# An RWKV-6 layer with a mixture-of-depths block: a rank sum, two early products and one PSUM bank moved

## The chip, the cores and the metric

The kernel runs on one core of one Trainium2 chip. The time is that of one execution on the device in microseconds. The profile is of one further execution and has a span of its own (205.5 us here), a little shorter than the time measured for the whole run.

## The reference, cut to what matters

There are two blocks, one after the other, all in fp32. The first is a linear attention with a decay for every element:

```python
for t in range(S):                       # B, H, S, D = 4, 8, 768, 48
    cur = einsum('bhd,bhe->bhde', u * k[t], v[t])
    y[t] = einsum('bhd,bhde->bhe', r[t], state + cur)
    state = w[t][..., None] * state + einsum('bhd,bhe->bhde', k[t], v[t])
```

Its output becomes x of shape (4, 768, 384). The second block scores each row, sends the 128 rows with the highest scores of each batch through a small network, and adds the result to them:

```python
scores = einsum('bsd,d->bs', x, w_gate)
top = argpartition(-scores[b], 128)[:128]
h = maximum(x[b, top] @ w1, 0)           # w1 384 x 1024
out[b, top] = x[b, top] + sigmoid(scores[b, top])[:, None] * (h @ w2)
```

All other rows of out are those of x.

## The kernel before, in words

The 768 steps of each batch are cut into 6 chunks of 128, so there are 24 chunks. Each chunk handles all 8 heads at once, two heads in the 128 partitions after a transpose. A chunk passes through these stages, each a small function:

- `decays_t` and `scans`: TensorE transposes w (ps_w), and two scans on DVE turn it into running products of the decays, to the right (`right`) and to the left (`left`) of each step.
- `inputs_t` and `scaled`: TensorE transposes k and r into PSUM (ps_t), and DVE multiplies them by `right` and `left`. The products are called K and R. `first_left` on ACT sets one column of `left`.
- `scores`, `masked`, `outputs_t`: K against R (ps_s), a mask on DVE (sc), then sc against v and the carried state against R (ps_yt), which ACT copies out as yt.
- `back`, `carry_products`, `carry`: K is transposed back, copied by ACT (kt), and multiplied with v (ps_kv) into the state that the next chunk needs.
- `own_products`, `own_weights`, `own_values`, `own_results`: the term of each step with itself, on POOL and ACT (rk, own, vo).
- `rows_out`, `row_products`, `row_sums`: yt is transposed into rows (ps_y), vo is added, the row goes out, and its score is summed.
- `compared`: each row's score is compared with those of the other rows of its batch (`ahead`, in bf16), and DVE leaves three counts a row in `lost`: its own comparisons in columns 0 and 1, and a fixed count of later rows in column 2.

When the last chunk of a batch is compared, `mixture(b)` finds each row's rank. 21 bf16 matmuls (L504) sum `ahead` over the partitions with weight -1 into a PSUM tile ps_r; one fp32 matmul with the identity (L509) adds `lost` to it; DVE sums three columns into `rank` (L514). Six comparisons make `pick`, a matmul turns it into row numbers (ps_i, idx), and POOL gathers the rows by an indirect DMA (xe). They are transposed (ps_x, xeT). `forward` is the network: ps_h over two halves of four blocks, each copied by ACT with a Relu into `hid` (L596), then ps_f = hid times w2 in 8 accumulating products (L602), then DVE's `ye` (L609) and an indirect DMA out (L612).

The order of the instructions on each engine is written out by hand. `turn(i)` works on several chunks at once: the scans of chunk i+2, K and R of chunk i+1, scores and outputs of chunk i, rows of chunk i-1. `mix` and `fed` insert pieces of `mixture` and `forward` between them. Each engine runs its own list in order, and waits on the others by semaphores. After the last turn the remaining pieces follow one another; the list `ended` marks this.

PSUM is full: psT holds two tiles and psW, psY, psK and psM one each, and psS one double tile. A tile can be written again when its last reader is done. In `forward`, after the turns, the first half of ps_h takes psY and the second half psM (L587); ps_f takes psM (L600). `warm(n)` runs n matmuls on zeros in psM, which keeps TensorE busy while the first loads arrive.

Of the kernel before, what the change touches and what calls it, by code (L numbers as in the profile page):

```python
# [10 lines left out]
FP32 = mybir.dt.float32  # L11
# [4 lines left out]
ALU = mybir.AluOpType  # L16
AX = mybir.AxisListType

L = 128
# [19 lines left out]
def kernel(  # L39
# [271 lines left out]
    def scaled(t, name, by):  # L311
        out = t[name] = lev.tile([L, HP, L], FP32, tag=name, name=name)
        nc.vector.tensor_mul(out, t.pop(name + "t"), t.pop(by))  # L313

    def own_products(t):
        n = t["n"]
        rk = t["rk"] = lev.tile([L, H, D], FP32, tag="rk", name="rk")
        nc.gpsimd.tensor_mul(rk, r_bufs[n % NBUF][:, :, 0:D], k_bufs[n % NBUF][:, :, 0:D])  # L318
# [172 lines left out]
    def mixture(b):  # L491

        every, ahead, lost = against[b]
        pool, tag = (psK, "kv") if ended else (psY, "y")  # L500
        ps = pool.tile([L, NCH, 3], FP32, tag=tag, name="ps_r")
        for e in range(NCH):
            for c in range(e + 1):
                nc.tensor.matmul(  # L504
                    ps[:, c, 0:1], ahead[:, e, c * L:(c + 1) * L], minus,
                    start=(e == 0), stop=False, skip_group_check=True,
                )
        against.pop(b)
        nc.tensor.matmul(  # L509
            ps.rearrange("p c k -> p (c k)"), ident, lost.rearrange("p c k -> p (c k)"),  # L510
            start=False, stop=True, skip_group_check=True,
        )
        rank = mod.tile([L, NCH], FP32, name="rank", bufs=2)
        nc.vector.tensor_reduce(out=rank, in_=ps, axis=AX.X, op=ALU.add)  # L514

        for gi, (c0, n) in enumerate(groups):

            pick = mod.tile([L, NCH, L], BF16, name="pick")
            at = rank
            if c0 > 0:  # L520
                at = mod.tile([L, NCH], FP32, name="at")
                nc.vector.tensor_scalar_add(out=at, in0=rank, scalar1=float(-c0))
            for c in range(NCH):
                nc.vector.tensor_scalar(
                    out=pick[:, c, :], in0=slots, scalar1=at[:, c:c + 1], scalar2=None,
                    op0=ALU.is_equal,
                )
            yield "half"
            ps = psK.tile([L, 2], FP32, tag="kv", name="ps_i")
            for c in range(NCH):  # L530
                nc.tensor.matmul(
                    ps, pick[:, c, :], ids[:, b, c, :], start=(c == 0), stop=(c == NCH - 1)
                )
            while len(picked) + len(feed) > 1:
                fed(1)
            idx = mod.tile([L, 1], UINT32, name="idx", bufs=2)
            nc.vector.tensor_scalar(
                out=idx, in0=ps[:, 0:1], scalar1=ps[:, 1:2], scalar2=float(b * S),
                op0=ALU.add, op1=ALU.max,
            )  # L540
            rows = views[b][0:b + 1].rearrange("b s c -> (b s) c")
            where = bass.IndirectOffsetOnAxis(ap=idx[0:n, 0:1], axis=0)
            xe = mod.tile([L, C], FP32, name="xe", bufs=2)
            if n < L:
                nc.vector.memset(xe, 0.0)
            nc.gpsimd.indirect_dma_start(
                out=xe[0:n], out_offset=None, in_=rows, in_offset=where,
                bounds_check=(b + 1) * S - 1, oob_is_err=False,
            )
            yield "end"  # L550
            yield "mid"

            ps = psT.tile([L, NDC, L], FP32, tag="t", name="ps_x")
            for dc in range(NDC):
                nc.tensor.transpose(ps[:, dc, :], xe[:, dc * L:(dc + 1) * L], ident)  # L555
            xeT = mod.tile([L, NDC, L], FP32, name="xeT", bufs=2)
            nc.scalar.copy(out=xeT, in_=ps)  # L557
            gate = mod.tile([L, 1], FP32, name="gate", bufs=2)
            gated = []
            picked.append((b, n, idx, xe, xeT, gate, gated))  # L560
            yield "end"


            scr = mod.tile([L, C], FP32, name="scr_x")
            nc.gpsimd.tensor_mul(scr, xe, wg_bc)
            yield "half"
            own = mod.tile([L, 1], FP32, name="own", bufs=2)
            nc.scalar.activation(out=scr, in_=scr, func=AF.Copy, accum_out=own)
            nc.scalar.activation(out=own, in_=own, func=AF.Exp, scale=-1.0)  # L569
            yield "end"  # L570
            nc.vector.tensor_scalar(
                out=gate, in0=own, scalar1=1.0, scalar2=3e38, op0=ALU.add, op1=ALU.min
            )
            nc.vector.reciprocal(out=gate, in_=gate)
            gated.append(True)
            yield "end"

    def forward(b, n, idx, xe, xeT, gate, gated):

        load_weights(len(weights) - NFC // 2)
        hid = mod.tile([L, NFC, L], FP32, name="hid")
        for f0 in range(0, NFC, 4):

            pool, tag = (psY, "y") if ended and f0 % 8 == 0 else (psM, "m")  # L587
            ps = pool.tile([L, 4, L], FP32, tag=tag, name="ps_h")
            for q in range(4):
                for dc in range(NDC):  # L590
                    nc.tensor.matmul(  # L591
                        ps[:, q, :], w1[:, dc, (f0 + q) * L:(f0 + q + 1) * L],
                        xeT[:, dc, :], start=(dc == 0), stop=(dc == NDC - 1),
                    )
                if q == 3:
                    nc.scalar.activation(out=hid[:, f0:f0 + 4, :], in_=ps, func=AF.Relu)  # L596
                yield q == 3

        load_weights(len(weights))
        ps = psM.tile([L, C], FP32, tag="m", name="ps_f")  # L600
        for fc in range(NFC):
            nc.tensor.matmul(  # L602
                ps, hid[:, fc, :], w2[:, fc, :], start=(fc == 0), stop=(fc == NFC - 1)
            )
            yield fc == NFC - 1
        while not gated:
            mix()
        ye = mod.tile([L, C], FP32, name="ye", bufs=2)
        nc.vector.scalar_tensor_tensor(  # L609
            out=ye, in0=ps, scalar=gate, in1=xe, op0=ALU.mult, op1=ALU.add  # L610
        )
        nc.gpsimd.indirect_dma_start(  # L612
            out=views[b][0:b + 1].rearrange("b s c -> (b s) c"),
            out_offset=bass.IndirectOffsetOnAxis(ap=idx[0:n, 0:1], axis=0),
            in_=ye[0:n], in_offset=None,
            bounds_check=(b + 1) * S - 1, oob_is_err=False,
        )
        yield True
# [46 lines left out]
    def turn(i):  # L665
        soon = i >= N - 1
        step(first_left, i + 1)
        step(own_products, i + 1)
        step(scores, i)
        step(own_values, i)  # L670
        step(carry, i - 1, work.get(i))
        step(scaled, i + 1, "K", "right")
        step(own_weights, i + 1)
        if soon:
            step(masked, i)
        if i == N - 1:
            sums.extend(check_sums())
        if i < N:
            step(compared, i - 2)
        if not soon:  # L680
            step(masked, i)
        step(back, i)
        if i == 0:
            warm(6)
        mix(place="half")
        step(rows_out, i - 1, soon)
        step(row_scores_soon if soon else row_products, i - 1)
        step(own_results, i)
        fed_in_turn(PIECES // 2, 2 if i >= N - 1 else 1)
        step(inputs_t, i + 1, "R", r_bufs)  # L690
        if i == -1:
            warm(4)
        step(scaled, i + 1, "R", "left")
        step(decays_t, i + 2)
        mix(place="mid")
        if i == -2:
            warm(2)
        step(range_check, i + 2)
        step(outputs_t, i)
        step(carry_products, i)  # L700
        fed_in_turn(PIECES - PIECES // 2, 1 if i == N - 1 else 0)
        if i == N - 1:
            step(compared, i - 1)
        step(inputs_t, i + 2, "K", k_bufs)
        if i == -2:
            warm(1)
        if not soon:
            step(row_sums, i - 1)
        step(scans, i + 2)
        if 0 <= i - 2 < N - 1 and chunks[i - 2][1] == NCH - 1:  # L710
            mixing.append([mixture(chunks[i - 2][0]), "end"])
        mix(place="end")
        if i > -2:
            loads(i + 5)
        if i in WEIGHT_TURNS:
            load_weights(1)
# [93 lines left out]
```

## Time and profile before

The time was 207.15 us, the median of three runs (207.13 to 207.45).

| engine | busy us of the 205.5 us span | instructions |
|---|---|---|
| TensorE matmul (PE) | 192.5 | 2303 |
| TensorE weight load (PEld) | 156.7 | 2303 |
| VectorE (DVE) | 161.2 | 350 |
| ScalarE (ACT) | 123.4 | 642 |
| GpSimd (POOL) | 133.2 | 165 |

A busy share is an average over the whole span. The start, some 16 us, is taken up by the first loads; then come the turns, until about 177 us; then the last two batches' networks. The profile has several views: the chain of work that ended last, which follows the span back from its end through whatever released each step; the timeline of each engine, with the start and length of each group of instructions and, in brackets, the idle time before it and what ended that; and groups of instructions by line and by tile.

### The profile page before, as it was taken

How to read it: one execution, taken by the hardware profiler on the slowest of the kernel's cores; microseconds unless marked ns; L12 is line 12 of the kernel's file. 1: busy time of each engine (PE TensorE's matmuls, PEld its weight loads, DVE VectorE, ACT ScalarE, POOL GpSimd, SP SyncE). 2: the span in 40 equal slices, each digit the busy share in tenths (PEclk: the TensorE clock that was granted, in tenths of full speed). 3: DMA queues.
4: the chain of work that ended last, by engine and by line, in shares of the span. 5: the costliest groups of instructions: out<-in, count | busy, mean ns of one | idle time of the engine just before them, and what ended most of it. 6: DMA issues, size and time to landing. Idle time of an engine off the chain costs nothing.

```text
span 205.5 us, 6424 instructions
## 1 busy us (share of the span) xinstructions
PE 192.5 (94%) x2303; PEld 156.7 (76%) x2303; DVE 161.2 (78%) x350; ACT 123.4 (60%) x642; POOL 133.2 (65%) x165
## 2 busy tenths in 40 slices
PE   7899999989899899999999999999999999999880
PEld 3568888868687688897887898897787898877740
DVE  5999999999999968989868888979868984941010
ACT  7177877768754866787445776786545776310300
POOL 6266898886858896669638898668738896122101
PEclk9999999999999999999999999999999999999997
DMA  5999999999999999988992894997553211101101
GB/s 109 186 163 179 165 180 211 221 205 143 249 178 257 201 183 217 236 193 182 210 158 80 153 217 94 137 171 150 124 83 91 56 49 41 48 33 40 40 6 43
DMA packets 105671, 29.20 MB, mean 142 GB/s; under 512 B 100512, under 2 KB 104864, under 8 KB 105632
## 3 DMA queue, kind: packets, MB, share of 16 engines
q1 hardware_dynamic: 105120, 27.14, 74.1%
q0 software_dynamic: 512, 1.57, 2.6%
q8 instruction: 20, 0.33, 0.7%
q14 instruction: 19, 0.16, 0.3%
HBM read 23.20 MB, written 5.51 MB: 140 GB/s over the span
## 4 chain that ended last, share of the span: by engine, by line
PE 81%; SPq 4%; DVE 4%; DMA 3%; ACT 2%; POOL 2%; issue 2%; POOLq 0%; DVEq 0%; ACTq 0%
PE ps_t L242 12%; PE ps_s L342 11%; PE ps_h L591 11%; PE ps_f L602 11%; PE ps_yt L375 10%; PE ps_yt L383 5%; PE ps_y L242 5%; PE ps_w L242 5%; PE ps_kv L437 5%; SPq L135 3%; PE ps_e L478 3%; DMA k_buf<-in_k_dram 3%; PE ps_r L504 1%; ACT rk L327 1%; PE ps_x L555 1%
## 5 line engine op out<-in xcount | busy, mean ns | idle before, releaser
L327 ACT ACTIVATE rk<-rk 128x48 f32<-128x48 f32 x192 | 43.7, 230 | 0.0
L327 ACT ACTIVATION_READ_ACCUMULATOR rk<-rk 128x1 f32 x192 | 36.2, 189 | 0.0
L407 POOL TENSOR_TENSOR x<-x,vo 128x384 f32<-128x384 f32 x22 | 22.1, 1006 | 21.2 <-ACT x L405 21.0
L266 DVE TENSOR_TENSOR_SCAN left<-ps_w,from_left 128x511 f32<-128x511 f32 x24 | 30.7, 1280 | 0.9
L388 ACT COPY yt<-ps_yt 128x512 f32<-128x512 f32 x24 | 14.1, 586 | 28.1 <-PE ps_yt L383 24.9
L255 DVE TENSOR_TENSOR_SCAN right_buf<-ps_w,from_right 128x511 f32<-128x511 f32 x24 | 29.1, 1210 | 1.7 <-PE ps_w L242 1.7
L350 DVE TENSOR_TENSOR sc<-ps_s,before_f 128x1024 f32<-128x1024 f32 x24 | 29.3, 1219 | 0.8 <-PE ps_s L342 0.8
L318 POOL TENSOR_TENSOR rk<-r_buf,k_buf 128x384 f32<-128x384 f32 x24 | 24.1, 1006 | 6.8 <-DMA r_buf<-in_r_dram 6.8
L342 PE MATMUL ps_s<-R,K 48*128 48x128 f32 x384 | 27.9, 285 | 0.3 <-ACT yt L388 0.2
L375 PE MATMUL ps_yt<-sc,v_buf 128*64 128x128 f32 x384 | 26.3, 278 | 1.4 <-PE ps_w L242 1.2
L342 PEld LDWEIGHTS ps_s<-R,K 48*128 48x128 f32 x384 | 23.3, 187 | 3.9 <-issue 2.7
L321 POOL TENSOR_TENSOR rk<-rk,u_bc 128x384 f32<-128x384 f32 x24 | 24.2, 1007 | 2.5 <-DMA u_bc<-in_u_dram 1.9
L591 PE MATMUL ps_h<-xeT,w 128*128 128x128 f32 x192 | 25.5, 280 | 0.2 <-ACT hid L596 0.2
L375 PEld LDWEIGHTS ps_yt<-sc,v_buf 128*64 128x64 f32 x384 | 20.6, 136 | 5.7 <-issue 2.7
L602 PE MATMUL ps_f<-w,hid 128*128 128x384 f32 x64 | 23.9, 500 | 0.7 <-ACT hid L596 0.7
L591 PEld LDWEIGHTS ps_h<-xeT,w 128*128 128x128 f32 x192 | 22.9, 192 | 1.6 <-ACT xeT L557 0.5
L412 POOL TENSOR_TENSOR scr<-x,wg_bc 128x384 f32<-128x384 f32 x22 | 22.0, 1001 | 1.7
L333 POOL TENSOR_TENSOR vo<-v_buf,own 128x384 f32<-128x384 f32 x24 | 20.0, 832 | 1.6 <-ACT rk L327 1.3
L313 DVE TENSOR_TENSOR K<-ps_t,right_buf 128x512 f32<-128x512 f32 x24 | 16.4, 682 | 4.9 <-PE ps_t L242 4.9
L313 DVE TENSOR_TENSOR R<-ps_t,left 128x512 f32<-128x512 f32 x24 | 16.5, 686 | 3.9 <-ACT own L569 1.6
L242 PE MATMUL ps_w<-ident,w_buf 128*128 128x128 f32 x96 | 15.3, 283 | 0.9 <-ACT every L489 0.7
L302 ACT ACTIVATE junk<-w_buf,high 128x384 f32<-128x384 f32 x24 | 15.1, 630 | 1.6 <-DMA w_buf<-in_w_dram 1.6
(102 smaller groups left out, 347.9 us busy)
## 6 DMA issues: line engine op xcount, KB each, us to landing
k_buf<-in_k_dram SPq DMA_DIRECT2D x24, 192.0 KB, 5.3
r_buf<-in_r_dram SPq DMA_DIRECT2D x24, 192.0 KB, 5.2
v_buf<-in_v_dram SPq DMA_DIRECT2D x24, 192.0 KB, 5.2
out_dram<-x SPq DMA_DIRECT2D x24, 192.0 KB, 3.1
w_buf<-in_w_dram SPq DMA_DIRECT2D x23, 192.0 KB, 4.6
w<-in_moe_w_dram SPq DMA_DIRECT2D x3, 512.0 KB, 5.2
w<-in_moe_w_dram SPq DMA_DIRECT2D x4, 384.0 KB, 5.4
w_buf<-in_w_dram SPq DMA_DIRECT2D x2, 96.0 KB, 2.8
```

The costliest lines, as they stand in the source:

```text
L242: nc.tensor.transpose(ps[:, j, :], src(j), ident)
L255: nc.vector.tensor_tensor_scan(out=flat[:, W - 2::-1], data0=wt[:, W - 1:0:-1], data1=from_right.rearrange("p j t -> p (j t)")[:, W - 2::- ...
L266: nc.vector.tensor_tensor_scan(out=left.rearrange("p j t -> p (j t)")[:, 1:W], data0=wt[:, 0:W - 1], data1=start.rearrange("p j t -> p (j ...
L313: nc.vector.tensor_mul(out, t.pop(name + "t"), t.pop(by))
L318: nc.gpsimd.tensor_mul(rk, r_bufs[n % NBUF][:, :, 0:D], k_bufs[n % NBUF][:, :, 0:D])
L321: nc.gpsimd.tensor_mul(t["rk"], t["rk"], u_bc)
L327: nc.scalar.activation(out=rk[:, h, :], in_=rk[:, h, :], func=AF.Copy, accum_out=o[:, h:h + 1])
L342: nc.tensor.matmul(ps[:, q, j, :], t["K"][rows, j, :], t["R"][rows, j, :], start=True, stop=True,)
L350: nc.vector.tensor_mul(t["sc"].rearrange("p q j t -> p (q j) t"), ps.rearrange("p q j t -> p (q j) t"), _heads(before_f, 2 * HP),)
L375: nc.tensor.matmul(ps[half(c), j % 2, j // 2, :], vt[:, 2 * j + q, :], t["sc"][:, q, j, :], start=(j < 2), stop=(old is None), skip_group_ ...
L591: nc.tensor.matmul(ps[:, q, :], w1[:, dc, (f0 + q) * L:(f0 + q + 1) * L], xeT[:, dc, :], start=(dc == 0), stop=(dc == NDC - 1),)
L602: nc.tensor.matmul(ps, hid[:, fc, :], w2[:, fc, :], start=(fc == 0), stop=(fc == NFC - 1))
```

## The change

There are four edits. The products K of the first two chunks are taken from DVE: ACT copies the transposed k out of PSUM, and POOL multiplies it. They are also issued earlier within the turn. The matmul that added `lost` goes; DVE sums `lost` by itself and then adds ps_r, which shrinks to one column a chunk and ends its accumulation with the last group of L504. The last batch's ps_f takes the psY bank in place of psM, so that it need not wait for the reader of the second ps_h. Two of the four warm matmuls ahead of the first chunk go. The arithmetic is the same.

```diff
+    def scaled_aside(t, name, by):
+        out = t[name] = lev.tile([L, HP, L], FP32, tag=name, name=name)
+        src = setup.tile([L, HP, L], FP32, name="src")
+        nc.scalar.copy(out=src, in_=t.pop(name + "t"))
+        nc.gpsimd.tensor_mul(out, src, t.pop(by))
...
-        ps = pool.tile([L, NCH, 3], FP32, tag=tag, name="ps_r")
+        ps = pool.tile([L, NCH], FP32, tag=tag, name="ps_r")
         for e in range(NCH):
             for c in range(e + 1):
                 nc.tensor.matmul(
-                    ps[:, c, 0:1], ahead[:, e, c * L:(c + 1) * L], minus,
-                    start=(e == 0), stop=False, skip_group_check=True,
+                    ps[:, c:c + 1], ahead[:, e, c * L:(c + 1) * L], minus,
+                    start=(e == 0), stop=(e == NCH - 1), skip_group_check=True,
                 )
         against.pop(b)
-        nc.tensor.matmul(
-            ps.rearrange("p c k -> p (c k)"), ident, lost.rearrange("p c k -> p (c k)"),
-            start=False, stop=True, skip_group_check=True,
-        )
         rank = mod.tile([L, NCH], FP32, name="rank", bufs=2)
-        nc.vector.tensor_reduce(out=rank, in_=ps, axis=AX.X, op=ALU.add)
+        nc.vector.tensor_reduce(out=rank, in_=lost, axis=AX.X, op=ALU.add)
+        nc.vector.tensor_add(rank, ps, rank)
...
-        ps = psM.tile([L, C], FP32, tag="m", name="ps_f")
+        pool, tag = (psY, "y") if b == B - 1 else (psM, "m")
+        ps = pool.tile([L, C], FP32, tag=tag, name="ps_f")
...
         step(first_left, i + 1)
+        if i < 1:
+            step(scaled_aside, i + 1, "K", "right")
         step(own_products, i + 1)
...
-        step(scaled, i + 1, "K", "right")
+        if i > 0:
+            step(scaled, i + 1, "K", "right")
...
         if i == -1:
-            warm(4)
+            warm(2)
```

## The prediction

> **What bounds the kernel now.** I read the chain that ended last first, because a busy share of 94% on PE does not say which stage sets the end.
>
> ```profile
> PE 81%; SPq 4%; DVE 4%; DMA 3%; ACT 2%; POOL 2%; issue 2%; POOLq 0%; DVEq 0%; ACTq 0%
> ```
>
> Four fifths of the chain is TensorE, so an edit pays where it takes matmul time out of the chain or closes a gap in it. The diff touches three places: the start, the four ranks (L501 to L514), and the last projection (L600). I therefore looked at each of these in time. First the start, from the chain in order of time (start, us, what), then DVE's timeline (start, us, instruction, idle before it).
>
> ```profile
> 10.29 5.35 DMA k_buf<-in_k_dram
> 15.78 0.63 PE ps_t L242 x4
> ```
>
> ```profile
> 7.78 0.67 DVE L313 TENSOR_TENSOR K<-ps_t,right_buf 128x512 f32<-128x512 f32 x1
> ...
> 11.88 0.67 DVE L313 TENSOR_TENSOR K<-ps_t,right_buf 128x512 f32<-128x512 f32 x1
> ...
> 23.64 0.35 DVE L484 SCALAR_TENSOR_TENSOR ahead<-ps_e,score,after_f 128x128 bf16<-128x128 f32 x1 [0.20 <-PE ps_e L478]
> ```
>
> The reader is to see two things. The transposes of the third chunk's k start when its load lands (10.29 + 5.35 = 15.64), and PE stood idle 0.50 us before them. From 15.78 on PE works without a gap. DVE is busy from 4.91 to 23.3, then waits 0.20 us for PE's ps_e: whatever lead it had won by 23.6 it would only have waited longer. Now a rank in the loop, on PE and on DVE:
>
> ```profile
> 104.25 0.67 PE L504 MATMUL ps_r<-minus,ahead 128*128 128x1 bf16 x21
> 104.78 0.38 PE L509 MATMUL ps_r<-lost,ident 128*128 128x18 f32 x2
> 105.09 1.16 PE L342 MATMUL ps_s<-R,K 48*128 48x128 f32 x16
> ```
>
> ```profile
> 58.21 1.28 DVE L266 TENSOR_TENSOR_SCAN left<-ps_w,from_left 128x511 f32<-128x511 f32 x1
> 59.79 0.18 DVE L514 TENSOR_REDUCE rank<-ps_r 128x6 f32<-128x18 f32 x1 [0.30 <-PE ps_r L509]
> 60.00 1.07 DVE L524 TENSOR_SCALAR pick<-slots,rank 128x128 bf16<-128x128 bf16 x6
> ```
>
> L509 holds PE from 104.78 to 105.09, 0.31 us, with PE dense before and after; DVE waits for it. At 59.79 DVE had run without idle since 23.64, so that one rank is on DVE's path more than on PE's. Last, the tail, PE then ACT then DVE:
>
> ```profile
> 187.69 5.62 PE L591 MATMUL ps_h<-xeT,w 128*128 128x128 f32 x48
> 194.00 5.43 PE L602 MATMUL ps_f<-w,hid 128*128 128x384 f32 x16 [0.69 <-ACT hid L596]
> ```
>
> ```profile
> 191.56 0.58 ACT L596 ACTIVATE hid<-ps_h 128x512 f32<-128x512 f32 x1
> 193.35 0.60 ACT L596 ACTIVATE hid<-ps_h 128x512 f32<-128x512 f32 x1 [1.21 <-PE ps_h L591]
> ```
>
> ```profile
> 199.46 0.62 DVE L609 SCALAR_TENSOR_TENSOR ye<-ps_f,gate,xe 128x384 f32<-128x384 f32 x1 [7.43 <-PE ps_f L602]
> ```
>
> ps_f sits 0.69 us behind the second hid, although its first four products need only the first hid, ready at 192.14. It waits because it takes the psM bank that the second ps_h is being read from. Everything after ps_f is serial.
>
> **What the Trainium skill says.** "GPSIMD Engine Reference", section 3.1, has GpSimd at 1.96 times VectorE's time for a fp32 tensor_tensor. The trace agrees: 1.006 us for 384 columns on POOL is 2.62 ns a column, 0.68 us for 512 on DVE is 1.33 ns, a ratio of 1.97. "PSUM — Partial Sum Buffer", "The four PSUM rules", says that GpSimd cannot touch PSUM, which is why the moved product needs a copy by ACT; and that last_mm has no observable effect on hardware, so moving stop=True to the last L504 matmuls costs nothing by that page (no run here shows it yet). "TensorE: Matmul & The Clock Gate", "What's actually happening", says the PE clock halves after an idle window of about 3.4 us; the windows of the trace show a granted clock of 1.00 throughout the first 20 us. The idle that the fewer warm matmuls can open is far shorter.
>
> **The change part by part.**
>
> *K of the first two chunks to ACT and POOL.* DVE loses two products of 0.67 us. ACT gains two copies 128x512 out of PSUM, 0.59 us each (row of yt, L388, 586 ns). POOL gains two products 128x512: not in the trace; lower bound one DVE product, 0.67, upper bound twice the 384-column row, 2.0; I take 1.006 x 512/384 = 1.34 us. K of chunk 0: ACT's first_left ends at 6.77, copy to 7.35, POOL to about 8.7, where DVE had it at 8.45; R comes at about 8.5 instead of 9.04, so the first ps_s can start at about 9.2 instead of 9.63. New waits: POOL waits for ACT's copy, with own_products and own_weights of the same chunk queued behind it (6.87 before, 8.7 now; own_weights waited for u_bc until 9.74 anyhow). For chunk 1 POOL is at K from about 10.9 to 12.3, its rk then at 13.3 and 14.4 and vo(0) at 15.2, where ACT asks for rk(1) at 15.99 and nobody needs vo(0) before 19.23. ACT's own_values(0), and with it kt(0), slip by about 0.3 us, to 13.4, and ps_kv(0) came at 14.65. All of it lies ahead of the k load that lands at 15.64. Before that, vo(0) shows that v of chunk 0 lands at 13.3, so ps_yt(0) (13.73 before) can gain 0.4 at most. **Value: 0 us**, at best 0.1 (ps_yt at 19.32 started about 0.09 after PE was free, behind DVE's sc).
>
> *warm(4) to warm(2).* Two matmuls, 1.03/4 = 0.26 us each, in the same DMA-bound stretch: **0 us**, hidden by the wait for k.
>
> *The rank without the identity matmul.* Four times L509 goes. Each holds PE 0.30 to 0.31 us by starts, 0.24 in the chain; I take 0.28 where PE is dense (104, 150). At 59 DVE decides: its reduce of lost starts when the left scan frees it (59.41, the usual 1.20 us after 58.21), the add follows 0.21 us later at 59.62 (distance of rank and pick, 59.79 to 60.00), since L504 ended by 59.52, and the picks start at 59.83 instead of 60.00: 0.17. In the tail the add starts after the last L504, about 181.06, and the picks at 181.27 instead of 181.51: 0.24; through idx this brings the gather forward by as much, and ps_x hangs on that gather (its weight load waited 0.36 for it), so 0.24 and not 0.30. The added DVE instruction (at least 0.16, the row of alls; at most 0.21 with its wait) is inside these figures; at 104 and 150 DVE sits idle 1.71 us ahead of the rank, which hides the reduce. Sum: 0.17 + 2 x 0.28 + 0.24 = **0.97 us**; ends 0.24 (tail only) and 4 x 0.31 = 1.24.
>
> *ps_f of the last batch in psY.* Its former tenant is the first ps_h, read by 192.14, so ps_f follows ps_h directly. Gain at least the 0.69 us idle, at most 0.85, because neighbours on PE overlap by about 0.16 (104.25 + 0.67 against 104.78, here 5.62 after 187.69 against a start at about 193.15). I take **0.78**. Product 5 needs the second hid at 193.95, and four products take 4 x 2 x 0.34 = 2.7 us: no wait.
>
> Sum: 0 + 0 + 0.97 + 0.78 = 1.75 us; 207.15 - 1.75 = **205.4 us**.
>
> **The rivals.**
>
> A. Only the tail pays: the ranks in the loop are caught up by another wait, as at 63 to 70, where the chain leaves PE for POOL, ACT and back, or by the loads, whose engines are at 9 tenths until slice 18. Against: the loop's chain is PE from 70.5 to 171.6, and POOL's long waits for loads end at 22.8. Then 207.15 - 0.24 - 0.78 = 206.1. Chance 0.12.
>
> B. The start pays too: DVE runs without idle from 23.64 to 59.5, and 2 x 0.67 us taken off it ahead of that would carry through to the end. Against: the 0.20 us idle at 23.64, and PE dense since the load. 205.4 - 1.2 = 204.2. Chance 0.04.
>
> C. Slower: fewer warm matmuls and later products let the granted clock fall in the start. Two windows of the skill's 3.4 us at half rate would add 3.4 us of matmul time, less about 0.9 us of slack (0.50 idle and 0.44 of warm work gone): 205.4 + 2.5 = 207.9. Against: the longest new PE gap that I can construct is about 1 us. With an unforeseen wait of ACT or POOL in the start counted in, 0.06.
>
> **How the numbers follow.** Forecast 0.78, A 0.12, B 0.04, C 0.06. The ends of the forecast's own terms: 0.69 + 0.75 (ranks 0.13 + 2 x 0.24 + 0.14) = 1.44 gives 205.7; 0.85 + 1.24 + 0.1 = 2.19 gives 205.0. With A at 206.1 taken in, and 0.2 for the measurement: 204.9 to 206.3. Faster by over 0.2% means under 206.74: 0.92; slower: 0.05; the same: 0.03.
>
> **What would show it.** Right: no L509, ps_f starting within 0.1 us of ps_h's end with a wait only ahead of its fifth product, if any; the k transposes still at about 15.8 with a longer PE idle before them; each rank's picks 0.17 to 0.3 us earlier against the work before them; POOL's 128x512 products near 1.34 us. Wrong: the k transposes move by more than 0.2 us either way, a granted clock under 1.00 before 24 us, or a new PE wait between 60 and 175 us that eats the 0.2 to 0.8 us gained by then.

## The result, and the profile after

The changed kernel takes 205.58 us (median of four runs, 205.12 to 205.87) against 207.14 us before: 1.56 us less, a ratio of 0.9921 with a 95% interval of 0.9899 to 0.9942. The forecast was 205.4 us. A second series of the same kernel gave 205.41 us against 207.32, ratio 0.9901 (0.9884 to 0.9919).

The chain that ended last is still TensorE in the main. It now passes through the load of the fourth chunk's k, with the issues ahead of it (SPq), and through a second k load in the loop (62.69 to 68.95):

```profile
PE 77%; SPq 7%; DMA 6%; DVE 4%; ACT 2%; issue 2%; POOL 0%; POOLq 0%; DVEq 0%; ACTq 0%
```

```profile
15.59 6.20 DMA k_buf<-in_k_dram
62.69 6.26 DMA k_buf<-in_k_dram
```

The second rank on PE's timeline (start, us, instruction). The identity matmul is missing, and ps_s follows L511 (the former L504) at 0.60 us, where it was 0.84 (104.25 to 105.09):

```profile
104.69 0.67 PE L511 MATMUL ps_r<-minus,ahead 128*128 128x1 bf16 x21
105.29 1.16 PE L349 MATMUL ps_s<-R,K 48*128 48x128 f32 x16
```

The first rank on DVE's timeline. The sum of lost runs at once behind the left scan, and the add starts 0.25 us after it; neither has a bracket, where the reduce before had one of 0.30. The picks start 1.64 us after the left scan did, where they started 1.79 after it (58.21 to 60.00):

```profile
58.52 1.28 DVE L266 TENSOR_TENSOR_SCAN left<-ps_w,from_left 128x511 f32<-128x511 f32 x1
59.71 0.14 DVE L517 TENSOR_REDUCE rank<-lost 128x6 f32<-128x18 f32 x1
59.96 0.17 DVE L518 TENSOR_TENSOR rank<-ps_r,rank 128x6 f32<-128x6 f32 x1
60.16 1.07 DVE L528 TENSOR_SCALAR pick<-slots,rank 128x128 bf16<-128x128 bf16 x6
```

The tail on PE, then the weight loads of ps_f, then ACT. The last ps_f has no wait in its bracket; its weights load at 192.72, under the last ps_h, and it starts before ACT has made the second hid (193.03 to 193.63):

```profile
187.37 5.62 PE L595 MATMUL ps_h<-xeT,w 128*128 128x128 f32 x48
192.83 5.33 PE L607 MATMUL ps_f<-w,hid 128*128 128x384 f32 x16
```

```profile
192.72 4.82 PEld L607 LDWEIGHTS ps_f<-w,hid 128*128 128x128 f32 x16
```

```profile
193.03 0.60 ACT L600 ACTIVATE hid<-ps_h 128x512 f32<-128x512 f32 x1 [1.22 <-PE ps_h L595]
```

The start on PE and POOL. The k transposes of the third and fourth chunk stand behind their loads, the third with a longer wait than before (0.75 against 0.50) and at the same time (15.82 against 15.78); the fourth came 0.31 us later than before (21.93 against 21.62). The K products on POOL take 1.27 us:

```profile
15.82 0.63 PE L242 MATMUL ps_t<-ident,k_buf 128*128 128x128 f32 x4 [0.75 <-DMA k_buf<-in_k_dram]
...
21.93 0.63 PE L242 MATMUL ps_t<-ident,k_buf 128*128 128x128 f32 x4 [0.19 <-DMA k_buf<-in_k_dram]
```

```profile
7.47 1.27 POOL L320 TENSOR_TENSOR K<-src,right_buf 128x512 f32<-128x512 f32 x1 [3.62 <-ACT src L319]
...
11.24 1.27 POOL L320 TENSOR_TENSOR K<-src,right_buf 128x512 f32<-128x512 f32 x1 [0.43 <-ACT src L319]
```

To see where time went, I compared the start of the same group in both traces: ps_s of each chunk, ps_h and ye of the last batch.

| from the start of | to the start of | before, us | after, us | difference |
|---|---|---|---|---|
| the span | third chunk's ps_s | 22.18 | 22.48 | +0.30 |
| third chunk's ps_s | eighth's | 29.52 | 29.53 | 0 |
| eighth's ps_s | tenth's (first rank) | 14.53 | 14.38 | -0.15 |
| tenth's ps_s | eleventh's (first gather) | 8.78 | 9.05 | +0.27 |
| fourteenth's ps_s | fifteenth's (second rank) | 8.62 | 8.38 | -0.24 |
| twentieth's ps_s | twenty-first's (third rank) | 8.62 | 8.37 | -0.25 |
| last ps_h half before the fourth rank (179.69, 179.62) | last batch's ps_h | 8.00 | 7.75 | -0.25 |
| last batch's ps_h | ye | 11.77 | 10.83 | -0.94 |

The gains add up to 1.83 us, the two lags to 0.57, which leaves the 1.26 us by which ye starts earlier (198.20 against 199.46); all else in between moved by less than 0.1. The profile thus raises three questions. Are the gains those of the two edits to which I put them? Is the start edit worth nothing? And do the two lags belong to the change?

### The profile page after: what moved, and what is told of

It reads as the page before. It is cut to its first block, busy times and chain, and to the rows that moved or that the text cites. A ratio compares the mean times of both kernels' runs of the same rounds, so it can differ in the third digit from the quotient of the medians.

```text
span 204.2 us, 6418 instructions
## 1 busy us (share of the span) xinstructions
PE 191.8 (94%) x2292; PEld 156.2 (76%) x2293; DVE 160.8 (79%) x352; ACT 124.6 (61%) x644; POOL 135.7 (66%) x167
## 4 chain that ended last, share of the span: by engine, by line
PE 77%; SPq 7%; DMA 6%; DVE 4%; ACT 2%; issue 2%; POOL 0%; POOLq 0%; DVEq 0%; ACTq 0%
PE ps_t L242 12%; PE ps_h L595 11%; PE ps_f L607 11%; PE ps_s L349 11%; PE ps_yt L382 10%; DMA k_buf<-in_k_dram 6%; SPq L135 5%; PE ps_yt L390 5%; PE ps_y L242 5%; PE ps_w L242 4%; PE ps_kv L444 4%; PE ps_e L485 3%; PE ps_r L511 1%; PE ps_x L559 1%; DVE left L266 1%
## 5 line engine op out<-in xcount | busy, mean ns | idle before, releaser
L349 PEld LDWEIGHTS ps_s<-R,K 48*128 48x128 f32 x384 | 23.3, 187 | 3.9 <-issue 2.7
L313 DVE TENSOR_TENSOR K<-ps_t,right_buf 128x512 f32<-128x512 f32 x22 | 15.0, 684 | 5.1 <-PE ps_t L242 5.1
L242 PE MATMUL ps_t<-ident,k_buf 128*128 128x128 f32 x96 | 15.4, 284 | 1.3 <-DMA k_buf<-in_k_dram 1.3
```

The lines of the kernel that those rows point to most:

```text
L242: nc.tensor.transpose(ps[:, j, :], src(j), ident)
L349: nc.tensor.matmul(ps[:, q, j, :], t["K"][rows, j, :], t["R"][rows, j, :], start=True, stop=True,)
```

## The experiments

All times are medians beside runs of the kernel before on the same chip, ratios with their 95% interval.

**Each edit by itself.** Three kernels with one edit each, and one with all but the start. The bank alone:

```diff
-        ps = psM.tile([L, C], FP32, tag="m", name="ps_f")
+        pool, tag = (psY, "y") if b == B - 1 else (psM, "m")
+        ps = pool.tile([L, C], FP32, tag=tag, name="ps_f")
```

> Before with the last ps_f alone moved to psY. If the bank alone made ps_f wait (my theory): 0.8 us less, 206.3, and PE's ps_f starts within 0.1 us of the end of ps_h. If the second hid is what ps_f waits for whatever the bank: no change, 207.1. If the change's gain came from the start: no change, 207.1.

Measured: 206.46 us against 207.27, ratio 0.9959 (0.9945 to 0.9972). In its trace ps_f follows ps_h without a wait. From ps_h to ye (198.68) it is 10.83 us as in the changed kernel, 0.94 less than before. The gain is the bank's.

```profile
187.85 5.62 PE L591 MATMUL ps_h<-xeT,w 128*128 128x128 f32 x48
193.31 5.33 PE L603 MATMUL ps_f<-w,hid 128*128 128x384 f32 x16
```

The rank alone:

```diff
-        nc.tensor.matmul(ps..., ident, lost..., start=False, stop=True)
-        nc.vector.tensor_reduce(out=rank, in_=ps, axis=AX.X, op=ALU.add)
+        nc.vector.tensor_reduce(out=rank, in_=lost, axis=AX.X, op=ALU.add)
+        nc.vector.tensor_add(rank, ps, rank)
```

> Before with the identity matmul of lost replaced by DVE's own sum and add, nothing else. My theory: four times about 0.24 us, 206.2, with each later group of PE earlier by that much. Rival A (the ranks in the loop are caught up by another wait): 0.24 us from the tail alone, 206.9. If the added DVE instruction costs as much as the matmul gives: 207.1.

Measured: 206.53 us against 207.27, ratio 0.9962 (0.9948 to 0.9975), 0.74 us less. From the third chunk's ps_s to ye it is 0.89 us shorter than before (22.73 to 199.12 against 22.18 to 199.46). The loop keeps its share, so rival A, with 0.24 from the tail alone, falls. At the first rank PE is 0.24 us earlier by the ninth ps_s, and 0.09 of it is gone by the tenth: the ps_i matmuls need DVE's picks, and they start 0.55 us behind the transposes of K (61.25 to 61.80), where it was 0.46 before (60.93 to 61.39). 0.15 stays.

```profile
59.40 0.67 PE L504 MATMUL ps_r<-minus,ahead 128*128 128x1 bf16 x21
60.00 1.16 PE L342 MATMUL ps_s<-R,K 48*128 48x128 f32 x16
...
61.25 0.60 PE L242 MATMUL ps_t<-ident,K 128*128 128x128 f32 x4
61.80 0.30 PE L528 MATMUL ps_i<-ids,pick 128*128 128x2 bf16 x6
```

The start alone, K of two chunks on ACT and POOL and warm(2):

> Before with K of the first two chunks on ACT and POOL and two warm matmuls fewer, rank and bank as before. My theory (the loads of k bound the start): 207.1, the k transposes of the third chunk at 15.8 as before with a longer wait ahead of them. Rival B (DVE's lead pays): 205.9. Third theory (the start edit costs something, since the k load of the fourth chunk and the first gather were 0.3 us each later in the changed kernel): 207.4 to 207.7.

Measured: 207.40 us against 207.27, ratio 1.0006 (0.9997 to 1.0014). No gain; the interval reaches from 0.1 us faster to 0.3 us slower, so a small loss, the lower edge of the third theory, is not excluded. From the third chunk's ps_s to ye its trace has 177.28 us (22.65 to 199.93), to a hundredth what the kernel before has. What happens to DVE's lead is seen where it waits for PE's first ps_e; it waits 0.35 us, the 0.20 that it waited before and 0.15 more:

```profile
23.07 0.68 DVE L313 TENSOR_TENSOR K<-ps_t,right_buf 128x512 f32<-128x512 f32 x1
24.10 0.35 DVE L491 SCALAR_TENSOR_TENSOR ahead<-ps_e,score,after_f 128x128 bf16<-128x128 f32 x1 [0.35 <-PE ps_e L485]
```

The change without the start (K on DVE for all chunks, warm(4)):

> The change without its start edit: rank and bank new, K on DVE and four warm matmuls as before. My theory: 205.4, the same as the whole change within 0.2 us, and the two lags of 0.3 us that the whole change showed are chance of the transfers, so they come and go between profiles. Third theory (the start edit costs): 205.0, faster than the whole change by 0.3 to 0.6 us. Rival B: 206.6, as the start's gain is missing.

Measured: 205.62 us against 207.27, ratio 0.9917 (0.9904 to 0.9931): the whole gain is there without the start edit. The single gains, 0.81 and 0.74, add up to 1.55, and both together give 1.65.

**Why the bank gains.** Here, in the kernel before, the last ps_f takes psY, but the eight products run in the order 4 to 7, 0 to 3, in every batch, so that the first needs the second hid.

```diff
-        for fc in range(NFC):
+        for m, fc in enumerate(list(range(NFC // 2, NFC)) + list(range(NFC // 2))):
```

A first kernel with this edit named the counter n, which is also the count of rows that ye writes back; it became 7 in place of 128.

> The last ps_f in psY as in the run with the bank alone, but every batch's eight products in the order 4 to 7, then 0 to 3, so that the first product needs the second hid. If the gain is that the first four products run while ACT makes the second hid (my theory): the gain is gone, 207.1 to 207.3, ps_f starts some 0.7 us after ps_h with a wait on hid. If the bank's former reader was all that held ps_f back and hid is ready anyway: 206.4 as with the bank alone.

It took 206.92 us against 207.13, with less to write back; I leave it out. With all rows written:

> As e5_late_half_first, whose edit also cut the rows written back by ye from 128 to 7 a batch (a loop variable stood for the row count), so that its time is not used; here all rows are written. My theory: the gain of the bank is gone, 207.0 to 207.3, ps_f starts 0.7 us after ps_h. If the bank alone matters: 206.4.

Measured: 207.13 us against 207.32, ratio 0.9993 (0.9985 to 1.0002). PE of this kernel:

```profile
187.57 5.62 PE L591 MATMUL ps_h<-xeT,w 128*128 128x128 f32 x48
193.88 5.43 PE L603 MATMUL ps_f<-w,hid 128*128 128x384 f32 x16 [0.69 <-ACT hid L596]
```

The wait of 0.69 us and the distance of 6.31 us from ps_h to ps_f are those of the kernel before. So a free bank gains nothing by itself; it gains because four products that need only the first hid can run in it while ACT makes the second.

**What one small fp32 matmul costs.** The kernel before, with L509 cut in two halves of nine columns (the code is shortened):

```diff
-        nc.tensor.matmul(ps (18 columns), ident, lost, ...)
+        for h in (0, 1):
+            nc.tensor.matmul(ps[:, half_c, :] (9 columns), ident, lost[:, half_c, :], ...)
```

> Before with the identity matmul of lost cut in two halves of nine columns, so four more small fp32 matmuls. If such a matmul costs its slot on PE whatever its columns (my theory): four times 0.24 to 0.31 us more, 208.1 to 208.5. If the loop absorbs it (rival A): 207.4 to 207.6. If cost went with columns: 207.2.

Measured: 208.23 us against 207.13, ratio 1.0053 (1.0040 to 1.0066). In the trace:

```profile
105.63 0.59 PE L511 MATMUL ps_r<-lost,ident 128*128 128x9 f32 x4
106.15 1.16 PE L342 MATMUL ps_s<-R,K 48*128 48x128 f32 x16
```

The distances across the ranks grow by 0.21 to 0.22 us each (8.83 against 8.62 at the second), 0.86 in all from the third chunk's ps_s to ye. That is under the 0.24 to 0.31 expected. The remaining 0.24 of the 1.10 us I can't place; in the start this trace stood 0.64 behind the one of before, the latest of the profiles compared below. A matmul of nine columns costs 0.21 to 0.22 where the one of eighteen gave 0.24 to 0.25 when it went, so most of the cost is the matmul's and not its columns', and the loop does not absorb it.

**Are the loads what holds the start?** The changed kernel with k and r of the third chunk and w of the fourth (the expectation below calls it the third's) ahead of v of the second, and k of the fourth ahead of the gate's weights:

```diff
+        if n > 3:
+            load(v_bufs, v, n - 2)
+        if n != 4:
+            load(k_bufs, k, n - 1)
...
     loads(3)
+    load(v_bufs, v, 1)
+    load(k_bufs, k, 3)
```

> The whole change with the same first loads in another order: k, r and w of the third chunk ahead of v of the second, and k of the fourth ahead of the gate's weights. If the loads bound the start (my theory): the k transposes of the third chunk come at about 15.1, when PE is free, and the time falls by 0.3 to 0.7 us, to 205.0. If PE or DVE bound it: no change, 205.6. If a later load takes over (v of the second chunk at about 18.6): 205.4 or more.

Measured: 205.48 us against 207.13, ratio 0.9926 (0.9913 to 0.9939). PE of this kernel:

```profile
14.99 0.66 PE L246 MATMUL ps_t<-ident,k_buf 128*128 128x128 f32 x4
...
19.21 1.09 PE L386 MATMUL ps_yt<-sc,v_buf 128*64 128x128 f32 x16 [0.42 <-DMA v_buf<-in_v_dram]
```

The k transposes come 0.8 us earlier, as soon as PE is free, and then v of the second chunk, now behind them in the queue, takes over. By the third chunk's ps_s 0.47 us is left (22.01 against 22.48), by the fourth's 0.25 (28.12 against 28.37). In the time nothing is seen: it gains 1.65 us, between the 1.56 and 1.91 of the changed kernel's two series. The same order without the start edit:

> The same order of loads, without the start edit (K on DVE, four warm matmuls; rank and bank as in the change). My theory: PE is free only at 15.3 to 15.4, and DVE holds the start once the load does not, so 205.3 against 205.0 with the start edit: there the start edit pays for the first time. If the start edit is worth nothing in any case: equal to the other within 0.1 us.

Measured: 205.31 us against 207.13, ratio 0.9912 (0.9899 to 0.9925). Its k transposes start at 15.21, 0.22 us after those with the start edit, and at the third chunk's ps_s it is level (21.96 against 22.01). Here the start edit does bring PE forward, for a moment, and the wait for v takes it back. My expectation that it would pay 0.3 us fails. It has the lowest median of the study, but its interval overlaps that of the change.

**Fewer bytes.** u and the gate's weights loaded as one row each, ahead of r of the first chunk, and spread by a matmul with ones and a copy by ACT:

```diff
-    nc.sync.dma_start(out=u_bc, in_=_rows(u, L))
+    nc.sync.dma_start(out=u_row, in_=_rows(u.rearrange("h d -> (h d)"), 1))
...
+        nc.tensor.matmul(ps, ones_row, row, start=True, stop=True)
+        nc.scalar.copy(out=to, in_=ps)
```

> The whole change, with u and the gate's weights loaded as one row each (1.5 KB in place of 192 KB) and spread over the partitions by a matmul with ones and a copy by ACT: two loads of 1.1 us less in the start. My theory (the loads bound the start): the k transposes of the third chunk come at about 15.0 with no wait, the fourth chunk's do not wait either, and with the loads out of the way DVE's lead counts: 0.6 to 0.9 us less than the whole change, 204.8. If engines bound the start: 205.6.

> The same small loads without the start edit (K on DVE, four warm matmuls). My theory: PE is free for the k transposes only at about 15.3, and DVE's order holds it, so 0.3 us behind the run with the start edit, 205.1. If the start edit is worth nothing even then: equal within 0.1 us, 204.8.

Measured: 206.24 and 206.15 us against 207.32, ratios 0.9938 (0.9920 to 0.9956) and 0.9940 (0.9925 to 0.9956): slower than the change by 0.6 to 0.8, against both expectations. For the kernel with the start edit PE shows why:

```profile
7.05 0.91 PE L244 MATMUL ps_b<-u_row,ones_row 1*128 1x384 f32 x2
...
10.46 1.16 PE L357 MATMUL ps_s<-R,K 48*128 48x128 f32 x16 [0.43 <-POOL K L328]
...
13.56 0.91 PE L244 MATMUL ps_b<-wg_row,ones_row 1*128 1x384 f32 x2
...
16.90 0.66 PE L250 MATMUL ps_t<-ident,k_buf 128*128 128x128 f32 x4
```

The k transposes no longer wait for a load, but PE gets to them only at 16.90: each spreading matmul holds PE for 0.84 us, from its start to that of the next group (13.56 to 14.40 for the second), and the copy of u stands ahead of first_left on ACT, which delays R, and K, as ps_s waits for POOL. Its third ps_s stands at 23.53, a full microsecond behind the 22.48 and 22.53 of the changed kernel. The load was removed and PE put in its place. Without the start edit PE came at 16.10, no later than the load allowed in a profile of the changed kernel below (16.16), and the third ps_s at 22.73, so this trace shows only about 0.2 us of that kernel's loss; the rest stays open. Whether the start edit pays once neither holds was not reached.

**Do the lags belong to the change?** The changed kernel once more:

> The changed kernel once more, for the two lags of 0.3 us that its profile showed. If they are chance of the transfers (my theory): the k transposes of the fourth chunk and the first gather's ps_x move by 0.2 to 0.4 us either way against the first profile, and the time is 205.4 to 205.7. If they belong to the change: both at the same place, 21.9 and 70.8.

Measured: 205.41 us, as said above. Now the third chunk's transposes are late (16.16, with a wait of 0.86) and the fourth's are at 21.94 with no wait of their own; ps_x follows ps_w by 0.49 us at the first gather, as before, where the first profile had 0.78:

```profile
70.07 0.66 PE L242 MATMUL ps_w<-ident,w_buf 128*128 128x128 f32 x4 [0.41 <-ACT every L496]
70.56 0.54 PE L559 MATMUL ps_x<-ident,xe 128*128 128x128 f32 x3
```

In the first profile that gather took 6.8 us to land, here 5.7, before 5.8. The distance of that lag, from the tenth ps_s to the eleventh, is 8.76 to 8.78 us in all seven other profiles of kernels with the new rank, and 9.05 in the first profile alone. So the lag at the gather came and went with a transfer. The one in the start is less clear: with the first loads in their old order, the third chunk's ps_s stood at 22.08, 22.18, 22.27, 22.34, 22.71, 22.73 and 22.82 in seven profiles without the start edit (22.18 is the kernel before), and at 22.48, 22.53 and 22.65 in three with it. The two sets overlap, so the 0.30 us can be chance, and three profiles are too few to exclude a small share of the edit. The times say the same. Against its partner without it, the start edit came out slower by 0.13 us alone, by 0.17 with k loaded first and by 0.09 with the small loads, and between 0.09 slower and 0.26 faster in the whole change: no gain, and a cost of about 0.1 us can't be told from none.

## Why the prediction was right

**The mechanism.** The two terms that were to pay did, each alone as in the sum. The two that were to pay nothing, K aside and the warm matmuls, paid nothing together; no run parts them. 1.75 us was forecast; the profile shows 1.83 us of gains. The two edits measured one by one add up to 1.55 us, together they gave 1.65, and the whole change 1.56 and 1.91. One sign of being wrong did show in the first profile, a new wait of PE between 60 and 175 us (0.27 at the first gather), but it belongs to that execution and not to the change.

**The rank**, forecast 0.97: 0.15 + 0.24 + 0.25 + 0.25 = 0.89 by the trace, 0.74 by the time. The first one was rightly put on DVE (0.17 forecast, 0.15 found). At 104 and 150 I took 0.28, between the distance of starts and the chain; the chain's 0.24 was right. L509 had started 0.53 us after L504 (104.25 to 104.78), but with L509 gone ps_s starts 0.60 after it, so not all of the 0.31 between the starts of L509 and ps_s came free. The doubled matmul points the same way: 0.21 to 0.22.

**The bank**, forecast 0.78, bounds 0.69 and 0.85: 0.94 by the trace, above the bound, and 0.81 by the time, whose interval holds both. 0.85 of it is the earlier start (ps_h to ps_f 5.46 us in place of 6.31). The other 0.10 I had not counted: the group is shorter, 5.33 in place of 5.43. Before, the weights and the first product started together at 194.00; now the weights load from 192.72, under ps_h.

```profile
194.00 4.81 PEld L602 LDWEIGHTS ps_f<-w,hid 128*128 128x128 f32 x16 [0.88 <-ACT hid L596]
```

**The start**, forecast 0: right. That the third chunk's k load held PE there was shown by the order of loads; with that load moved the edit still paid nothing in the time. One step of it was off: I had ps_s of the first chunk at 9.2 in place of 9.63; it stayed at 9.68, as the k transposes ahead of it waited 0.41 us for the second chunk's k. POOL's 128x512 product took 1.27 us (1.34 forecast), and K of the first chunk came at 8.74 (8.7 forecast). Two pages of the Trainium skill hold here: "GPSIMD Engine Reference", section 3.1, has 1.96 for the ratio to VectorE, and 1.27 us against 0.68 is 1.87; "PSUM — Partial Sum Buffer", "The four PSUM rules", says that last_mm, the flag of a group's last matmul, has no observable effect, and the 21 matmuls take 0.67 us as before with stop=True on the last of them.

Against rival C the prediction leaned on the granted clock, which reads 1.00 in the first 24 us of both kernels. That column does not settle it: it reads 1.00 too where TensorE is at half its pace. Four transposes took 1.06 us at 3.80, and 0.60 to 0.66 later. The slow pace ended at about 4.6 us in the profile of the start edit alone and at 7.1 in the first one of the change. Both kernels give PE the same matmuls up to there, so the change is not what moved it.

```profile
3.80 1.06 PE L242 MATMUL ps_w<-ident,w_buf 128*128 128x128 f32 x4
4.66 1.06 PE L236 MATMUL ps_n<-nothing 128*128 128x512 bf16 x2
5.68 1.09 PE L242 MATMUL ps_t<-ident,k_buf 128*128 128x128 f32 x4
...
8.08 0.63 PE L242 MATMUL ps_w<-ident,w_buf 128*128 128x128 f32 x4
```

What speaks against rival C is that behind 7.1 us every group of four transposes in the start takes 0.60 to 0.66 us in both kernels, with half the warm matmuls too.

**Loose readings**, none of which enters the sum: DVE was busy until 23.44, not 23.3. PE was not without a gap from 15.78 on; it had ten, of 0.17 to 0.53 us, between 42 and 70. ps_f did not start 0.69 us behind the second hid, but 0.05 (193.95 to 194.00), after PE had been idle for 0.69. The two warm matmuls are 0.52 us in one place and 0.44 in another; by starts they took 0.43 (7.32 to 8.18 for four).

**What was luck.** By the trace the rank term was 0.08 us too large and the bank term 0.16 too small, so the sum came out closer than its parts. Chance of the transfers, 0.74 us between profiles at the third chunk's ps_s, is nearly half of the gain. It sat in my range only because the range was 1.4 us wide for other reasons.

## What to carry to other kernels

When an engine is on the chain of the last work without a gap, price a removed matmul by the distance between its neighbours' starts on both sides, and check a second engine at each place: where DVE had run without idle, the same matmul was worth 0.15 us in place of 0.24. Expect somewhat less than the distance: here 0.24 of 0.31 came free. A wait on a PSUM bank pays to remove only if work can run in that time, so look at what the first instruction behind it needs. In a start held by loads, as here, edits to the engines only moved waits about, and when one load was moved the next in the queue had its turn.

## What the runs showed that I had not expected

A matmul that spreads one row of 384 fp32 columns over 128 partitions, with a contraction over a single partition, holds PE for 0.84 us, with 0.91 us of busy time. A ps_f product of as many columns, contracted over 128 partitions, holds it for 0.73 to 0.75 us where it stands alone between other groups (186.64 to 187.37 and 181.14 to 181.89 in the changed kernel), and for 0.65 to 0.68 us in a row of eight, so a contraction over one partition was no cheaper. Against it stands a load of 192 KB whose issue took 1.14 us: cheap on paper to remove, and dear where the replacement ran.
